# A gated scan feeding a top-1 mixture of experts, on one core: two-operand vector instructions cut in pieces, the start reordered, weights converted in independent parts

## The chip, the cores and the metric

One core of a Trainium2 chip runs the whole program. The metric is the device time of one execution in microseconds (us), as a median over runs. The engines are named as the profile names them: PE (TensorE, matrix multiplication), DVE (VectorE), ACT (ScalarE), POOL (GpSimd), SP (SyncE, which issues most transfers here). Every engine works through its own list of instructions strictly in order; semaphores tie the lists together.

## The reference

```python
# x, r_gate, i_gate: [4, 5056, 256], a_param: [256]
a_base = 1 / (1 + exp(-a_param)); sig_r, sig_i = sigmoid(r_gate), sigmoid(i_gate)
a_t = exp(8 * sig_r * log(clip(a_base, 1e-6, 1 - 1e-6)))          # the decay
x_gated = sqrt(maximum(1 - a_t * a_t, 1e-6)) * sig_i * x
for t in range(S):
    h = a_t[:, t] * h + x_gated[:, t];  y[:, t] = h                # the scan
# y as N = 20224 rows of 256; 8 experts, w1 [8, 256, 1024], w2 [8, 1024, 256]
logits = y @ w_gate + modality_bias[modality_id]                   # top-1 routing
e = argmax(logits);  gate = softmax(logits)[e]
out[row] = gate * (maximum(y[row] @ w1[e], 0) @ w2[e])
```

## The kernel before

**The work.** The scan runs over 23 chunks of time steps (`CHUNKS`): four of 128 steps, 17 of 256, one of 128, one of 64; a chunk holds its steps of all four batches, so chunk 4 and the later long ones give 1024 rows each. Per chunk: three loads `a`, `g`, `x` (the two gates and the input); on ACT two tanh (L507 on `a`, L495 on `g`), two exponentials (L512), a square (L516) and a square root (L518); on DVE the gating product (L498), the product with the root (L520), and the scan itself (L534, `tensor_tensor_scan` over all 2048 columns of a long chunk). Those three DVE instructions read two tensors from the on-chip memory. "Sizing" finds a power of two for the chunk: DVE takes maxima (L669, L678, L683 `mxy`), PE transposes them (L545 into `psz`), DVE and PE answer twice more (L548, L552, L556, L561). With it `y` is split into a high and a low half-precision part (L712 on ACT, L724 on DVE), PE forms the logits (L738, `psl`), DVE routes (L794 to L862, with three small matmuls L832 to L835 in between), SP transposes the rows (L763, `rt`), and POOL scatters them into a table by expert (L885, `rows<-rt,di`, 128 rows an instruction).

**Experts.** Rows are taken from the table in pages of 128 or 256 rows of one expert (`X<-rows` on SP). Below, P0, P1, P2 ... are the pages in PE's order; P0 and P1 have 128 rows, the others 256. Two pages are chosen at a time on DVE (`choose_two`, L985 to L997), one of each of the two experts that the modality bias makes most frequent. A page is layer one (L1197, groups of 12 matmuls into `ph`), ACT and DVE making the two parts of the hidden rows (L1138, L1140), layer two (L1239 into `po`), ACT scaling by the gate (L1149), and POOL writing 128 output rows (L1153). Layer one of a page alternates on PE with layer two of the page before.

**Weights.** The four matrices of the two frequent experts (w0 to w3) come in as f32 and are converted into a high and a low f16 part (`convert`): a scale (16 matmuls L321, then DVE), the high part on DVE (L352), the low part as two matmuls on PE (L368, L369, "a pair" below: four pairs a matrix, 16 in all) and a copy on ACT (L371). The other experts are handled at the end.

**What sets the order.** Nothing waits for a free engine at run time. A planner inside the kernel (`run`) simulates generators that yield (engine, estimated duration, condition, lag) and writes out every engine's list in the order of its own clock; a priority decides among requests that start nearly together. If an estimate is off, an instruction stands too early in its engine's list and all behind it wait. `count["pe"]` also ties each scatter to the last matmul planned ahead of it.

Of the kernel before, what the change touches and what calls it, by code (L numbers as in the profile page):

```python
# [40 lines left out]
HI = "DDDDAD"  # L41
LO = "PPPPDD"
START = "0 w w 1 w w 2"
W_AT = 11.5
C_STEP = 2
GROW = 1.01
EARLY = 8
# [3 lines left out]
W_STEP = 0.1  # L51
# [26 lines left out]
def kernel(  # L78
# [53 lines left out]
    nc.vector.tensor_scalar_add(ch, ch, 1.0)  # L132
    nc.vector.reciprocal(ch, ch)
    nc.vector.tensor_scalar(out=ch, in0=ch, scalar1=1e-6, scalar2=1.0 - 1e-6, op0=ALU.max, op1=ALU.min)
    nc.scalar.activation(ch, ch, AF.Ln)
# [91 lines left out]
    free = {"PE": 0.0, "ACT": 6.0, "DVE": 7.0, "POOL": 9.0, "DMA": 1.0, "queue": 1.0}  # L227
    threads = []
# [108 lines left out]
    def convert(k, name, raw, to, sc):  # L337

        if LO[k] == "P":
            yield "ACT", 0.2, room("dg")  # L340
            td = take("dg")
            dg = sm.tile([P, P], F32, name=f"dg{name}", tag="dg")
            nc.scalar.activation(dg, ident, AF.Copy, scale=sc)
        for v in range(2):
            vs = slice(FF * v, FF * v + FF)
            src, hi, lo = raw[:, vs], to[:, vs], to[:, 2 * FF + FF * v : 3 * FF + FF * v]
            if HI[k] == "A":
# [5 lines left out]
            if LO[k] == "G":  # L353
                yield "POOL", 1.9, None
                nc.gpsimd.tensor_scalar(out=src, in0=src, scalar1=sc, scalar2=None, op0=ALU.mult)
                yield "POOL", 1.9, None, 0.0
                nc.gpsimd.tensor_tensor(out=lo, in0=src, in1=hi, op=ALU.subtract)
                continue
            if LO[k] == "D":
                yield "DVE", 1.2, None  # L360
                nc.vector.scalar_tensor_tensor(out=lo, in0=src, scalar=sc, in1=hi, op0=ALU.mult, op1=ALU.subtract)
                continue
            for h in range(2):
                yield "PE", 1.25, room("ph"), 0.2
                tp = take("ph")
                us = slice(512 * h, 512 * h + 512)
                pl = psh.tile([P, 512], F32, name=f"pl{name}_{v}{h}", tag="ph")
                nc.tensor.matmul(pl, dg, src[:, us], start=True, stop=False)  # L368
# [27 lines left out]
    def hot_weights(m):  # L396
# [12 lines left out]
        yield from convert(m, f"{m}", raw, hw[e][w], sc)  # L409
        give("wr", tr)  # L410
        mark["w", m] = plan["end"]
        tiles["wiv", m] = iv
        if w == 1:
            yield "DVE", 0.07, seen(("w", m - 1)), 0.0
            nc.vector.tensor_tensor(out=hiv[e], in0=tiles["wiv", m - 1], in1=iv, op=ALU.mult)
            mark["hot", e] = plan["end"]

    def cold_weights(pg):
# [11 lines left out]
        for w in range(2):  # L430
# [4 lines left out]
            yield from convert(2 * HOT + w, f"c{pg.c}_{w}", raw[w], pg.w[w], sc)  # L435
            give("wr", t[w])
            if w == 0:
                iv0 = iv
        yield "DVE", 0.07, None, 0.0
# [46 lines left out]

    def done(c, name):

        give(*tickets[c, name])

    def gate_chunk(c):

        z = CHUNKS[c][1] / 256
        yield "ACT", 0.13 + 1.7 * z, seen(("load", c, "g"))
        nc.scalar.activation(tiles[c][1], tiles[c][1], AF.Tanh, scale=0.5)  # L495
        yield "DVE", 0.09 + 2.12 * z, seen(("load", c, "x"))
        a, g, x = tiles[c]
        nc.vector.scalar_tensor_tensor(out=g, in0=g, scalar=1.0, in1=x, op0=ALU.add, op1=ALU.mult)  # L498
        mark["gated", c] = plan["end"]

    def scan_chunk(c):
# [3 lines left out]
        yield "ACT", 0.13 + 1.7 * z, seen(("load", c, "a"))  # L505
        a = tiles[c][0]
        nc.scalar.activation(a, a, AF.Tanh, scale=0.5)  # L507
# [9 lines left out]
        yield "ACT", 0.13 + 1.7 * z + 2.56, None  # L517
        nc.scalar.activation(s, s, AF.Sqrt, scale=-0.25, bias=quarter)  # L518
        yield "DVE", 0.09 + 2.12 * z, None
        nc.vector.scalar_tensor_tensor(out=g, in0=s, scalar=0.5e-3, in1=g, op0=ALU.max, op1=ALU.mult)  # L520
# [12 lines left out]
        yield "DVE", 0.08 + 4.26 * z, None  # L533
        nc.vector.tensor_tensor_scan(out=g, data0=a, data1=g, initial=0.0, op0=ALU.mult, op1=ALU.add)  # L534
# [7 lines left out]
    def power_of_two(name, mx, ng, ps, sc, iv, lag=0.2):  # L542

        yield "PE", 0.06, None
# [4 lines left out]
        yield "DVE", 0.1, None, lag  # L549
# [5 lines left out]
        yield "PE", 0.06 * nd / ng, None  # L555
# [106 lines left out]
    def size_chunk(c):  # L662
# [24 lines left out]
        yield "SP", 0.0, allof(room("lg"), seen("gate")), 0.0  # L687
        tl = take("lg")
# [3 lines left out]
        yield from power_of_two(f"y{c}", mx, B, ps, sc, iv)  # L692
# [172 lines left out]
    def gates(c, l):  # L865
# [3 lines left out]
        yield "ACT", 0.2, None  # L869
# [473 lines left out]
```

## Time and profile before

| | |
|---|---|
| runs | 980.01, 982.94 (median), 983.73 us |
| the profiled execution | 987.79 us, of which the span 986.0 us; 4.85 us above the median |
| busy in the span | PE 919.5 us (93%), DVE 662.3 (67%), ACT 578.6 (59%), POOL 485.1 (49%) |
| PE clock granted | 0.981 of full speed as a mean |
| first matmul of a page (P0) / of the first full page (P2) | 45.88 us / 74.40 us |
| start of the last chunk's scan / of the last row scatter | 645.7 us / 670.8 us |

In the timelines a row gives its start in us, its duration in us, engine, line, operation, output and inputs, how many instructions are merged, and in brackets the idle time of the engine ahead of it and what ended that. In the tables of waits a row gives who waited for whom, the total in us, how often, and the longest. In the tables of one line's instructions stand the number, then the durations in ns as minimum / median / maximum, then the first and last start.

### The profile page before, as it was taken

What the parts mean: (1) busy time and instruction counts of PE and PEld (TensorE: products, weight loads), DVE (VectorE), ACT (ScalarE), POOL (GpSimd) and SP (SyncE); (2) the same over time, 40 slices, a digit from 0 to 9 for tenths busy, and PEclk for the clock granted to TensorE, in tenths of its full rate; (3) what the DMA queues carried; (4) which work ended last, traced back from release to release, by engine and by line L of the source; (5) the groups of instructions that cost most, each with busy time, mean ns of one, the idle gap of its engine ahead of it and who ended that gap; (6) DMA issues with size and microseconds to landing.
All of it is one profiled execution on the core that took longest, in us unless ns stands there. A gap on an engine that the chain in (4) does not pass through costs nothing. (4 is left out here: it accounts for less than half of the span.)

```text
span 986.0 us, 22341 instructions
## 1 busy us (share of the span) xinstructions
PE 919.5 (93%) x8516; PEld 791.1 (80%) x8516; DVE 662.3 (67%) x1564; ACT 578.6 (59%) x819; POOL 485.1 (49%) x539
## 2 busy tenths in 40 slices
PE   3779897899899999999999999999999999999997
PEld 2358686688688888888888888888889888888886
DVE  5888796787899999898888997863523332232321
ACT  7698666575877777775877857643333333333332
POOL 7333563656565777675756767553451111111111
PEclk9899998899999999999999999999999999999999
DMA  7767865678798888877798877644431212212110
GB/s 284 215 204 176 243 218 114 213 192 217 189 252 213 258 235 210 193 200 167 227 247 203 239 175 204 130 113 112 127 92 49 57 49 53 51 49 55 49 39 18
DMA packets 221734, 156.10 MB, mean 158 GB/s; under 512 B 198129, under 2 KB 201330, under 8 KB 215090
## 3 DMA queue, kind: packets, MB, share of 16 engines
q1 hardware_dynamic: 205296, 110.61, 45.7%
q0 software_dynamic: 16176, 43.98, 12.6%
q8 instruction: 68, 1.11, 0.5%
q14 instruction: 48, 0.39, 0.1%
q10 hardware_dynamic: 146, 0.00, 0.0%
HBM read 68.76 MB, written 44.35 MB: 115 GB/s over the span
## 5 line engine op out<-in xcount | busy, mean ns | idle before, releaser
L1197 PE MATMUL ph<-X,hw 128*128 128x256 f16 (+1 forms) x3936 | 480.7, 273 | 8.2 <-DMA X<-rows 8.0
L1239 PE MATMUL po<-hw,H 128*128 128x256 f16 x3840 | 474.2, 274 | 2.3 <-DVE H L1140 1.7
L1197 PEld LDWEIGHTS <-hw 128*128 128x128 f16 x3936 | 379.8, 99 | 59.4 <-DMA X<-rows 8.8
L1239 PEld LDWEIGHTS <-H 128*128 128x128 f16 x3864 | 375.5, 98 | 49.9 <-DVE H L1140 2.5
L1140 DVE SCALAR_TENSOR_TENSOR H<-ph,H 128x512 f16<-128x512 f32 (+1 forms) x332 | 219.2, 668 | 249.8 <-ACT H L1138 198.4
L1138 ACT ACTIVATE H<-ph 128x512 f16<-128x512 f32 (+1 forms) x332 | 191.2, 580 | 275.3 <-PE ph L1197 255.5
L1153 POOL DMA_INDIRECT out_dram<-ot,mt x161 | 197.3, 1226 | 307.0 <-ACT ot L1149 251.9
L885 POOL DMA_INDIRECT rows<-rt,di x158 | 211.8, 1341 | 156.5 <-PE po L1239 50.9
L1149 ACT ACTIVATE ot<-po,gt 128x256 f32<-128x256 f32 x161 | 75.9, 471 | 76.0 <-PE po L1239 51.5
L534 DVE TENSOR_TENSOR_SCAN g<-a,g 128x2048 f32<-128x2048 f32 (+2 forms) x23 | 88.0, 3824 | 0.8
L712 ACT ACTIVATE a<-g,scy 128x512 f16<-128x512 f32 (+2 forms) x92 | 55.8, 655 | 7.4 <-DVE g L534 7.3
L724 DVE SCALAR_TENSOR_TENSOR a<-g,scy,a 128x512 f16<-128x512 f32 (+2 forms) x92 | 58.1, 667 | 0.9 <-ACT a L712 0.9
L512 ACT ACTIVATE a<-a,ch 128x1024 f32<-128x1024 f32 (+2 forms) x46 | 50.5, 1116 | 0.2
L520 DVE SCALAR_TENSOR_TENSOR g<-x,g 128x2048 f32<-128x2048 f32 (+2 forms) x23 | 45.5, 1980 | 2.6 <-ACT x L518 2.5
L498 DVE SCALAR_TENSOR_TENSOR g<-g,x 128x2048 f32<-128x2048 f32 (+2 forms) x23 | 45.9, 1994 | 1.1 <-ACT g L495 1.1
L669 DVE TENSOR_REDUCE top<-x 128x4 f32<-128x2048 f32 (+2 forms) x23 | 45.3, 1971 | 0.4 <-DMA x<-in_x_dram 0.4
L507 ACT ACTIVATE a<-a 128x2048 f32<-128x2048 f32 (+2 forms) x23 | 38.3, 1667 | 8.3 <-DMA a<-in_r_gate_dram 8.2
L516 ACT ACTIVATE x<-a 128x2048 f32<-128x2048 f32 (+2 forms) x23 | 38.4, 1669 | 7.3 <-DVE g L498 7.1
L518 ACT ACTIVATE x<-x,quarter 128x2048 f32<-128x2048 f32 (+2 forms) x23 | 40.5, 1761 | 0.3
L495 ACT ACTIVATE g<-g 128x2048 f32<-128x2048 f32 (+2 forms) x23 | 38.3, 1663 | 1.1 <-DMA g<-in_i_gate_dram 1.0
L518 ACT ACT_TABLE_LOAD x22 | 28.2, 1283 | 0.5
L885 POOL DMA_INDIRECT rows<-nt,ni x16 | 15.5, 972 | 20.8 <-PE po L1239 10.4
(194 smaller groups left out, 464.7 us busy)
## 6 DMA issues: line engine op xcount, KB each, us to landing
a<-in_r_gate_dram SPq DMA_DIRECT2D x17, 1024.0 KB
g<-in_i_gate_dram SPq DMA_DIRECT2D x17, 1024.0 KB
x<-in_x_dram SPq DMA_DIRECT2D x17, 1024.0 KB
wr<-in_moe_w_dram SPq DMA_DIRECT2D x4, 1024.0 KB
out_dram<-ot,mt POOLq DMA_INDIRECT x161
a<-in_r_gate_dram SPq DMA_DIRECT2D x5, 512.0 KB
g<-in_i_gate_dram SPq DMA_DIRECT2D x5, 512.0 KB
x<-in_x_dram SPq DMA_DIRECT2D x5, 512.0 KB
```

Of the source, the lines that this page charges most:

```text
L512: nc.scalar.activation(sl, sl, AF.Exp, scale=ch[:, h : h + 1], bias=ch[:, h : h + 1])
L518: nc.scalar.activation(s, s, AF.Sqrt, scale=-0.25, bias=quarter)
L534: nc.vector.tensor_tensor_scan(out=g, data0=a, data1=g, initial=0.0, op0=ALU.mult, op1=ALU.add)
L712: nc.scalar.activation(ys[:, 0, :, g], yg[:, :, g, :].rearrange("p h (k b) -> p h k b", b=Q), AF.Copy, scale=sc[:, g : g + 1])
L724: nc.vector.scalar_tensor_tensor(out=ys[:, 1, :, g], in0=yg[:, :, g, :].rearrange("p h (k b) -> p h k b", b=Q), scalar=sc[:, g : g + 1], i ...
L885: ins = nc.gpsimd.indirect_dma_start(out=rows[:, :], out_offset=bass.IndirectOffsetOnAxis(ap=idx, axis=0), in_=src, in_offset=None, bounds ...
L1138: nc.scalar.activation(t.H[:, 0, hs, :], ph[:, :, 0:st], AF.Relu)
L1140: nc.vector.scalar_tensor_tensor(out=t.H[:, 1, hs, :], in0=ph[:, :, 0:st], scalar=0.0, in1=t.H[:, 0, hs, :], op0=ALU.max, op1=ALU.subtract,)
L1149: nc.scalar.activation(t.ot[:, a, :], po, AF.Copy, scale=t.gt[:, a : a + 1])
L1153: ins = nc.gpsimd.indirect_dma_start(out=out[:, :], out_offset=bass.IndirectOffsetOnAxis(ap=t.mt[:, a, 0:1], axis=0), in_=t.ot[:, a, :], i ...
L1197: ins = nc.tensor.matmul(ph[:, v, 0:st], lhsT, rhs, start=(m == 0), stop=(m == len(mm) - 1))
L1239: ins = nc.tensor.matmul(po, lhsT, rhs, start=(f == 0 and m == 0), stop=(f == NF - 1 and m == len(mm) - 1))
```

## The change

1. `pieces` and `piece`: from chunk 1 on the DVE instructions with two tensor inputs are cut: the two products in 2, the scan in 4 for a long chunk (1 and 2 for a short one). The planner records these (`held`) and plans a POOL instruction that would start inside one for its end.
2. The start: the tanh of chunk 0 stands ahead of the logarithm of the decay (`decay()`); the bias is loaded ahead of `a_param`; the expert order is computed ahead of `ch`; chunk 1 is loaded ahead of w1 (`START`); the modality order starts at 15 instead of 9 on the planner's clock.
3. Weights: the high parts of w0 and of half of w2 go to ACT (`HI`); each quarter of a low part is a thread of its own (`low(u)`), urgent; the low part of the rare experts' second matrix is cut in four.
4. Planner costs: a table load on ACT (1.28) only where the table changes; a lag of 3.0 (1.0 for chunks 2 to 6) ahead of both of PE's steps in sizing (`SIZE_LAG`); dearer small steps.

```diff
-HI = "DDDDAD"
+HI = ["A", "D", "AD", "D", "A", "D"]
-START = "0 w w 1 w w 2"
+START = "0 w 1 w w w 2"
+MODALITY = 15.0
+SIZE_LAG = 3.0
-W_STEP = 0.1
+W_RANK = [0.0, 0.3, 0.3, 0.6]
...
-    nc.scalar.activation(ch, ch, AF.Ln)
...
+    def decay():
+        yield "ACT", 0.2, seen(("tanh", 0, "a"), ("tanh", 0, "g")), None, "L"
+        nc.scalar.activation(ch, ch, AF.Ln)
...
+                if eng == "POOL":
+                    for b0, b1 in held:
+                        if b0 - 0.1 <= th.start < b1 - 0.1:
+                            th.start = b1 - 0.1
...
+            if eng == "ACT" and len(th.req) > 4 and th.req[4] != table[0]:
+                table[0], dur = th.req[4], dur + 1.28
...
+        def low(u):
+            us = slice(512 * u, 512 * u + 512)
+            src, hi, lo = raw[:, us], to[:, us], to[:, 2 * FF + 512 * u : 2 * FF + 512 * u + 512]
...
+                yield "PE", 1.25, room("ph")
...
             for h in range(2):
-                yield "PE", 1.25, room("ph"), 0.2
...
+                add(low(2 * v + h), prio, plan["end"] + 0.2, urgent)
...
+    def pieces(c, k):
+        return max(1, CHUNKS[c][1] * k // P) if c else 1
+    def piece(t, i, n):
+        w = t.shape[1] // n
+        return t[:, i * w : (i + 1) * w]
...
-        yield "DVE", 0.08 + 4.26 * z, None
-        nc.vector.tensor_tensor_scan(out=g, data0=a, data1=g, initial=0.0, op0=ALU.mult, op1=ALU.add)
+        n = pieces(c, 2)
+        for i in range(n):
+            yield "DVE", 0.08 + 4.26 * z / n, None, 0.0 if i else None, True
+            ai, gi = piece(a, i, n), piece(g, i, n)
+            nc.vector.tensor_tensor_scan(out=gi, data0=ai, data1=gi, initial=0.0, op0=ALU.mult, op1=ALU.add)
...
-    def power_of_two(name, mx, ng, ps, sc, iv, lag=0.2):
-        yield "PE", 0.06, None
+    def power_of_two(name, mx, ng, ps, sc, iv, lag=None):
+        yield "PE", 0.1, None, lag
...
+        lag = SIZE_LAG if c > 6 else SIZE_LAG / 3 if c > 1 else None
...
-    add(modality_order(), (0, 9), 9.0)
+    add(decay(), (0, 0))
+    add(modality_order(), (0, 9), MODALITY)
...
-        add(hot_weights(m), (2, W_AT + W_STEP * m))
+        add(hot_weights(m), (2, W_AT + W_RANK[m]), urgent=True)
```

In the main part DVE gets 1648 instructions instead of 1558 (the scan 78 instead of 23, the two products 40 each instead of 23, the low part of the rare experts' matrix 8 instead of 4, the high parts three fewer), ACT three more; PE, POOL and SP keep theirs. Lines of the changed kernel are some 20 to 50 higher: L507 is L550, L495 is L535, L512 L556, L516 L560, L534 L584, L545 L595, L683 L733, L738 L789, L885 L936, L985 L1036, L1138 L1189, L1153 L1204, L1197 L1248, L1239 L1290, L368 L382, L369 L383.

ACT at the very start, before: `a_246`, `g_248` and `x_250` are chunk 0's tiles, `pm` and `mq` belong to the modality order.

```order
L114 ACT_TABLE_LOAD
L114 ACTIVATE ch<-cpar 128x2
L135 ACT_TABLE_LOAD
L135 ACTIVATE ch<-ch 128x2
L507 ACT_TABLE_LOAD
L507 ACTIVATE a_246<-a_246 128x1024
L512 ACTIVATE a_246<-a_246,ch 128x512 x2
L495 ACTIVATE g_248<-g_248 128x1024
L613 ACTIVATE mq<-pm_281 128x316
L613 ACTIVATE mq<-pm_302 128x316
L516 ACTIVATE x_250<-a_246 128x1024
L518 ACT_TABLE_LOAD
```

The same stretch of ACT after:

```order
L116 ACT_TABLE_LOAD
L116 ACTIVATE ch<-cpar 128x2
L550 ACTIVATE a_241<-a_241 128x1024
L535 ACTIVATE g_243<-g_243 128x1024
L162 ACT_TABLE_LOAD
L162 ACTIVATE ch<-ch 128x2
L556 ACT_TABLE_LOAD
L556 ACTIVATE a_241<-a_241,ch 128x512 x2
L560 ACTIVATE x_245<-a_241 128x1024
L562 ACT_TABLE_LOAD
L562 ACTIVATE x_245<-x_245,quarter 128x1024
```

Both tanh moved ahead of the logarithm and its table, and the two copies of the modality order left the way of the square.

PE where the first page begins, before: `pl` are the pairs of the low parts (`wr_412` is w2), `ph_0_708` is the first group of P0.

```order
L368 MATMUL pl_11_680<-wr_291,dg_472 128x512
L369 LDWEIGHTS nid
L369 MATMUL pl_11_680<-hw_1_225,nid 128x512
L368 MATMUL pl_00_703<-wr_412,dg_668 128x512
L369 LDWEIGHTS nid
L369 MATMUL pl_00_703<-hw_0_226,nid 128x512
L1197 LDWEIGHTS hw_0_224
L1197 MATMUL ph_0_708<-X_664,hw_0_224 128x128
```

PE where the first page begins, after: `wr_420` is w3, `pl_3` its last quarter.

```order
L595 MATMUL psz_774<-identb,mxy_736 4x128
L382 MATMUL pl_2_780<-wr_420,dg_695 128x512
L383 LDWEIGHTS nid
L383 MATMUL pl_2_780<-hw_1_222,nid 128x512
L382 MATMUL pl_3_790<-wr_420,dg_695 128x512
L383 LDWEIGHTS nid
L383 MATMUL pl_3_790<-hw_1_222,nid 128x512
L1248 LDWEIGHTS hw_0_219
L1248 MATMUL ph_0_808<-X_689,hw_0_219 128x128
```

Seven pairs that stood among the matmuls of P0 and P1 now stand ahead of P0: all 16 pairs come first. Chunk 1's logits (`psl`) stand behind 14 pairs instead of 12.

POOL around the rows of chunk 4, before: `rt_0_1806` are its rows, `ot_...` the output rows of pages.

```order
L769 TENSOR_SCALAR rt_0_1806<-tid 128x8
L1153 DMA out_dram<-ot_1885,mt_1450 20224x256
L885 DMA rows<-rt_0_1806,di_1974 164096x258 x3
L1153 DMA out_dram<-ot_1885,mt_1450 20224x256
L885 DMA rows<-rt_0_1806,di_1974 164096x258 x5
L1153 DMA out_dram<-ot_2078,mt_1770 20224x256 x2
```

The same place on POOL after (`rt_0_1902` is chunk 4):

```order
L820 TENSOR_SCALAR rt_0_1902<-tid 128x8
L936 DMA rows<-rt_0_1902,di_2051 164096x258 x4
L1204 DMA out_dram<-ot_2055,mt_1873 20224x256
L936 DMA rows<-rt_0_1902,di_2051 164096x258 x3
L1204 DMA out_dram<-ot_2055,mt_1873 20224x256
L1204 DMA out_dram<-ot_2194,mt_1953 20224x256
L936 DMA rows<-rt_0_1902,di_2051 164096x258
```

Three output writes now stand among the eight row scatters, where one stood.

More of the change, by code (lines that the diff above doesn't have):

```diff
@@ L226 @@
     slots = {t: Slots(n) for t, n in BUFS.items()}
-    free = {"PE": 0.0, "ACT": 6.0, "DVE": 7.0, "POOL": 9.0, "DMA": 1.0, "queue": 1.0}
-    threads = []
+    free = {"PE": 0.0, "ACT": 5.2, "DVE": 7.5, "POOL": 9.0, "DMA": 1.0, "queue": 1.0}
+    threads, held, table = [], [], ["E"]
     plan = {"end": 0.0}
@@ L284, in run @@
             dur = th.req[1]
+            if eng == "ACT" and len(th.req) > 4 and th.req[4] != table[0]:
+                table[0], dur = th.req[4], dur + 1.28
             end = th.start + dur
             free[eng] = end
+            if eng == "DVE" and len(th.req) > 4:
+                held.append((th.start, end))
+                del held[:-4]
             if eng == "DMA":
@@ L408, in hot_weights, with then @@
         yield from scale_of(f"{m}", raw, sc, iv, FACTOR[w])
-        yield from convert(m, f"{m}", raw, hw[e][w], sc)
-        give("wr", tr)
-        mark["w", m] = plan["end"]
         tiles["wiv", m] = iv
+        def then():
+            give("wr", tr)
+            mark["w", m] = plan["end"]
+        yield from convert(m, f"{m}", raw, hw[e][w], sc, (2, W_AT + W_RANK[m]), True, then)
         if w == 1:
@@ L434, in cold_weights, with then @@
             yield from scale_of(f"c{pg.c}_{w}", raw[w], sc, iv, FACTOR[w])
-            yield from convert(2 * HOT + w, f"c{pg.c}_{w}", raw[w], pg.w[w], sc)
-            give("wr", t[w])
+            def then(w=w):
+                give("wr", t[w])
+                mark["cw", pg.c, w] = plan["end"]
+            yield from convert(2 * HOT + w, f"c{pg.c}_{w}", raw[w], pg.w[w], sc, (1, 3), False, then)
             if w == 0:
                 iv0 = iv
-        yield "DVE", 0.07, None, 0.0
+        yield "DVE", 0.07, seen(("cw", pg.c, 0), ("cw", pg.c, 1)), 0.0
         pg.inv = sm.tile([P, 1], F32, name=f"pinv{pg.c}", tag="pinv", bufs=3)
@@ L493, in gate_chunk @@
         z = CHUNKS[c][1] / 256
-        yield "ACT", 0.13 + 1.7 * z, seen(("load", c, "g"))
+        yield "ACT", 0.13 + 1.7 * z, seen(("load", c, "g")), None, "E"
         nc.scalar.activation(tiles[c][1], tiles[c][1], AF.Tanh, scale=0.5)
-        yield "DVE", 0.09 + 2.12 * z, seen(("load", c, "x"))
-        a, g, x = tiles[c]
-        nc.vector.scalar_tensor_tensor(out=g, in0=g, scalar=1.0, in1=x, op0=ALU.add, op1=ALU.mult)
+        mark["tanh", c, "g"] = plan["end"]
+        n = pieces(c, 1)
+        for i in range(n):
+            yield "DVE", 0.09 + 2.12 * z / n, seen(("load", c, "x")), 0.0 if i else None, True
+            a, g, x = [piece(t, i, n) for t in tiles[c]]
+            nc.vector.scalar_tensor_tensor(out=g, in0=g, scalar=1.0, in1=x, op0=ALU.add, op1=ALU.mult)
         mark["gated", c] = plan["end"]
@@ L516, in scan_chunk @@
         nc.scalar.activation(s, a, AF.Square)
-        yield "ACT", 0.13 + 1.7 * z + 2.56, None
+        yield "ACT", 0.13 + 1.7 * z, None, None, "S"
         nc.scalar.activation(s, s, AF.Sqrt, scale=-0.25, bias=quarter)
-        yield "DVE", 0.09 + 2.12 * z, None
-        nc.vector.scalar_tensor_tensor(out=g, in0=s, scalar=0.5e-3, in1=g, op0=ALU.max, op1=ALU.mult)
+        n = pieces(c, 1)
+        for i in range(n):
+            yield "DVE", 0.09 + 2.12 * z / n, None, 0.0 if i else None, True
+            gi, si = piece(g, i, n), piece(s, i, n)
+            nc.vector.scalar_tensor_tensor(out=gi, in0=si, scalar=0.5e-3, in1=gi, op0=ALU.max, op1=ALU.mult)
         done(c, "x")
```

99 lines of the change are left out of this document (53 added, 46 removed).

## The prediction

> **What bounds it.** I read the page first, then PE's table of waits by stretches, then the timelines around the long waits.
>
> ```profile
> PE 919.5 (93%) x8516; PEld 791.1 (80%) x8516; DVE 662.3 (67%) x1564; ACT 578.6 (59%) x819; POOL 485.1 (49%) x539
> ```
>
> PE is the bound of the whole. What can be won is PE's waiting, and what the clock loses behind a wait. The matmuls of pages come in groups of 12, and at full rate they keep a spacing that this stretch shows, as does the slow rate behind a wait:
>
> ```profile
> 45.88 1.48 PE L1197 MATMUL ph<-X,hw 128*128 128x128 f16 x12
> ...
> 52.21 0.41 PE L738 MATMUL psl<-a,wg 128*32 128x128 f16 x16
> ...
> 74.40 8.44 PE L1197 MATMUL ph<-X,hw 128*128 128x256 f16 x60 [1.82 <-DMA X<-rows]
> ...
> 134.64 1.47 PE L1197 MATMUL ph<-X,hw 128*128 128x256 f16 x12
> 135.95 1.47 PE L1239 MATMUL po<-hw,H 128*128 128x256 f16 x12
> ...
> 141.19 6.71 PE L1239 MATMUL po<-hw,H 128*128 128x256 f16 x60
> 153.82 9.66 PE L1197 MATMUL ph<-X,hw 128*128 128x256 f16 x60 [5.91 <-DMA X<-rows]
> ...
> 188.06 0.16 PE L556 MATMUL psz<-dmy,onesb 4*128 4x4 bf16 x1 [3.45 <-issue]
> ...
> 188.18 2.74 PE L1197 MATMUL ph<-X,hw 128*128 128x256 f16 x12
> ...
> 193.27 1.83 PE L1197 MATMUL ph<-X,hw 128*128 128x256 f16 x12
> ```
>
> A group is 1.31 us (135.95 - 134.64). P2 begins at 74.40. P8 begins at 153.82 after 5.91 us without rows, and its first 60 matmuls take 9.66 us where 60 took 6.71 just before: a long wait costs about 3 us more. From P8 on PE is nearly closed, so whatever P8 gains stays to the end. PE's waits between these points and after:
>
> ```profile
> PE ph L1197 <- DMA X<-rows: 6.2, 2, 5.9
> PE psl L738 <- ACT a L712: 2.5, 4, 0.8
> ```
>
> That is 75 to 160 us; from 160 to 700 us it is sizing:
>
> ```profile
> PE psz L545 <- DVE mxy L683: 7.7, 8, 1.6
> PE psz L556 <- issue: 3.6, 2, 3.4
> PE psz L545 <- DVE lm L678: 3.2, 1, 3.2
> PE psz L556 <- DVE dmy L552: 2.6, 5, 0.8
> ```
>
> The 3.4 is the wait at 188.06, and it is no wait of the order: ACT and DVE resume in the same instant, all three put down to no work on this core.
>
> ```profile
> 187.43 0.60 ACT L1138 ACTIVATE H<-ph 128x512 f16<-128x512 f32 x1 [4.14 <-remote]
> 187.47 0.28 DVE L548 TENSOR_REDUCE m1y<-psz 4x1 f32<-4x128 f32 x1 [3.11 <-remote]
> ```
>
> I take it for a pause of this one execution: 3.45 us, and 2.5 behind it (24 matmuls from 188.18 to 193.27, 5.09 instead of 2.62): 6 us, close to the 4.85 by which the profiled execution stands above the median.
>
> **The start, up to P2: 1 us won at most, counted as part of the next term.** Chunk 0's root is limited by ACT:
>
> ```profile
> 4.83 0.20 ACT L114 ACTIVATE ch<-cpar 128x2 f32<-128x2 f32 x1 [1.72 <-DMA cpar<-in_a_param_dram]
> ...
> 7.86 1.06 ACT L507 ACTIVATE a<-a 128x1024 f32<-128x1024 f32 x1
> 8.95 1.52 ACT L512 ACTIVATE a<-a,ch 128x512 f32<-128x512 f32 x2
> ...
> 14.17 1.05 ACT L516 ACTIVATE x<-a 128x1024 f32<-128x1024 f32 x1
> 15.30 1.28 ACT L518 ACT_TABLE_LOAD   x1
> 16.59 1.15 ACT L518 ACTIVATE x<-x,quarter 128x1024 f32<-128x1024 f32 x1
> ```
>
> After: the exponential at 5.3 (a_param now comes second), two tanh of 1.06, a table, the logarithm, a table (1.28, 0.20, 1.28), the two exponentials 1.52, the square 1.05, a table 1.28: the root starts at 14.2, 2.4 us earlier. But P2 hangs on chunk 1, not on chunk 0, and chunk 1's logits stood behind 12 pairs on PE at 52.21 and now stand behind 14, with fewer page matmuls (36 short ones, 2 us) ahead. From about 29.5 us (chunk 0's routing must answer first) 13 pairs follow, at the 1.5 us that two pairs here are apart:
>
> ```profile
> 35.57 1.12 PE L368 MATMUL pl<-wr,dg 128*128 128x512 f32 x2
> ...
> 37.12 1.10 PE L368 MATMUL pl<-wr,dg 128*128 128x512 f32 x2
> ...
> 41.61 1.91 PE L368 MATMUL pl<-wr,dg 128*128 128x512 f32 x2
> ```
>
> 13 x 1.55 and 2 us for w3's and the scales' matmuls give 51.7: the same time. P0 then starts at about 55 instead of 45.88, and the choice of P2 stands on DVE behind P0's and P1's hidden rows and chunk 2's root. I put that choice at 68.5 to 70, where it was:
>
> ```profile
> 69.24 0.20 DVE L985 TENSOR_TENSOR d<-b,u 1x2 f32<-1x2 f32 x1
> ```
>
> The rows arrive some 5 us later in both, so P2 at 73 to 75. Bounds: -5 us if the lead of chunk 0 comes through, +8 if pairs go at the rate of 41.61 (1.91 for two passes instead of 1.1; 13 x 0.6 = 8). The high parts moved to ACT cost 3 x 1.1 there, in ACT's waits for pairs, and relieve DVE; changed `START` delays w1 by 1.5 MB of loads, which nothing waits for before its pairs.
>
> **P2 to P8: 2 us won.** P8 needs chunk 4's rows, which POOL scatters:
>
> ```profile
> 129.84 3.21 POOL L885 DMA_INDIRECT rows<-rt,di  x1 [1.66 <-DVE m1y L548]
> ...
> 137.21 2.08 POOL L885 DMA_INDIRECT rows<-rt,di  x1 [0.30 <-issue]
> 139.59 1.90 POOL L885 DMA_INDIRECT rows<-rt,di  x1 [0.30 <-issue]
> 141.79 0.98 POOL L885 DMA_INDIRECT rows<-rt,di  x1 [0.30 <-issue]
> ...
> 144.37 4.34 POOL L885 DMA_INDIRECT rows<-rt,di  x1 [0.31 <-issue]
> ```
>
> A free scatter takes 0.98, the four long ones 7.6 us more in all. The long ones end 0.8 to 0.9 us after a DVE instruction of two inputs:
>
> ```profile
> 138.35 2.28 DVE L520 SCALAR_TENSOR_TENSOR g<-x,g 128x2048 f32<-128x2048 f32 x1
> ...
> 143.49 4.42 DVE L534 TENSOR_TENSOR_SCAN g<-a,g 128x2048 f32<-128x2048 f32 x1
> ```
>
> 144.37 + 4.34 is 0.80 after the scan's end, 139.59 + 1.90 is 0.86 after L520's. The scatter of 137.21 got through where one such instruction follows on another (it ended at 139.29, inside L520). So a piece should let a scatter through at its end, and the loss per hit falls to a piece's 1.2 us. I take 3 of the 7.6 as left. But two more output writes, taken at a free scatter's 1.29 (0.98 and the 0.30 ahead of it), now stand among the eight: the stretch of 18.9 us becomes 11 x 1.29 + 3 = 17.2. The chunk's logits stood on PE ahead of P6 and still do; its rows start at about 128 instead of 129.84, P8 at 151.5. PE is ready for P8 earlier, since the stalls at chunk 4's logits (2.5) go (their matmuls stand 6.6 instead of 3.9 us of page work behind the last split), and so waits longer there: what is won before P8 is lost at P8. Bounds: 10 won (next part), 8 lost.
>
> **Sizing after P8: 5 us won.** The lag moves PE's two steps back in its list. Counted in groups between the page whose hidden rows stand just ahead of DVE's step and PE's step, the 16 chunks from 7 on have 45 for the first step and 46 for the second before, 50 and 54 after: 14% more, up for some chunks and down for others. Of the 13.5 us (7.7, 3.2, 2.6) and about 1.5 at the slow rate behind the 3.2, I take a third. Bounds: 0 and 15.
>
> **More DVE work: nothing.** A scan of 512 columns takes 1.22, of 2048 4.42; a product of 1024 1.21, of 2048 2.28:
>
> ```profile
> L534 DVE TENSOR_TENSOR_SCAN g<-a,g x23: 1224/4424/4426, 20.2 to 645.7; 128x2048 f32<-128x2048 f32 x17, 128x1024 f32<-128x1024 f32 x5, 128x512 f32<-128x512 f32 x1
> ```
>
> ```profile
> L498 DVE SCALAR_TENSOR_TENSOR g<-g,x x23: 684/2282/2423, 11.4 to 634.6; 128x2048 f32<-128x2048 f32 x17, 128x1024 f32<-128x1024 f32 x5, 128x512 f32<-128x512 f32 x1
> ```
>
> ```profile
> L498 DVE SCALAR_TENSOR_TENSOR g<-g,x 128x1024 f32<-128x1024 f32 x5 | 6.1, 1215 | 1.1 <-ACT g L495 1.1
> ```
>
> 17 x (0.47 + 2 x 0.15) is 13 us on DVE. Between 200 and 650 us DVE has 53 us free:
>
> ```profile
> 200.00:650.00 450.00, 432.71 (x4109) 376.01 (x4107) 396.53 (x886) 330.43 (x435) 300.24 (x259) 1.00 0.79 207
> ```
>
> So it is covered, and a hidden-row step (L1140) no longer stands behind a whole scan; if the cover were gone, PE would wait for L1140.
>
> A rule speaks against the pieces. The Trainium skill ("SBUF — State Buffer", on the shared port pair) says that a DVE instruction with two inputs from that memory and a GpSimd instruction that reads it take the pair as an exclusive lock for a whole instruction, and that whoever comes second blocks fully. By the rule POOL would hold up DVE as well. The trace shows only the one side: L520 at 138.35 kept its 2.28 with a scatter under way, and no scan of 2048 took more than 4426 ns. By the rule the sum would be that of the last rival below; by the trace it stays.
>
> **The sum**, against the profiled execution's own 987.8: -6 for the pause, -2 to P8, -5 in sizing, 0 for DVE: 975, which is 8 under the median of the runs.
>
> **Rivals.**
> - The early lead comes through: P2 3 us earlier, all 7.6 of blocked scatters gone, so P8 10.6 earlier, the wait and the slow rate behind it (3) gone: 987.8 - 6 - 13.6 - 5 = 963. For it: the chain to P8 is a chain of waits, no engine is full there. Against: the choice of P2 stands late, output writes stand among the rows.
> - It does not do what it says: the waits only move, nothing won before P8 or in sizing: 982, the median. For it: the margins in PE's list rise by only 14%, for some chunks they fall.
> - Slower: all pairs ahead of P0, at the slow rate. P2 moves by 8, chunk 4's logits stand in PE's list behind P5, so P8 moves as well: 987.8 - 6 + 8 = 990. It decides if pairs are more than 1.9 apart. For it: PE waits for chunk 0's routing right ahead of them, and went slow behind the wait at 41.61.
> - Slower by DVE: POOL is busy two thirds of the time (300 of 450). If each of 90 more starts waited half a scatter (0.49), DVE would lose 0.67 x 90 x 0.49 = 30 of its 53 free us, and sizing's 13.5 us of waits would grow as the free time shrinks, to 31: 987.8 - 6 - 2 + 17 = 997.
>
> **Chances.** Faster by over 0.5% is under 978.0, slower over 987.9 (about what these runs can tell from no change). The forecast 0.46 (969 to 981: 0.34 faster, 0.12 same), the lead that comes through 0.22, waits that only move 0.15, slow pairs 0.14, the held DVE 0.03. So faster 0.56, same 0.27, slower 0.17. The range 960 to 990 leaves out the lower end of the first rival (0.05), the upper half of the third (0.07) and the last.
>
> **What would show it.** The root of chunk 0 (L562) near 14 us; 16 pairs ahead of P0 at about 55, 1.5 us apart; P2 at 73 to 75; P8 at about 151 with a wait of 8 or more ahead of it; scatters of at most 2.2 us; waits for `mxy`, `lm` and `dmy` of about 9 us in all; DVE busy up by 13. Wrong if P2 comes before 71 or after 78, if P8's wait is gone, or if a scan piece takes much over 1.22.

## The result and the profile after

The changed kernel takes 971.75 us (median of five runs, 969.54 to 975.64); the kernel before has 980.76 in its five. The ratio is 0.9904, 95% interval 0.9874 to 0.9933: faster by 1%. The profiled execution of the changed kernel took 970.82, 17 less than the profiled one before; 6 of these 17 are the pause, which the changed kernel's trace does not have.

The lines of the page that answer to those of before: busy time of the engines, and row scatters and output writes on POOL (busy, mean of one in ns, idle time before). The two POOL lines of before first:

```profile
L1153 POOL DMA_INDIRECT out_dram<-ot,mt x161 | 197.3, 1226 | 307.0 <-ACT ot L1149 251.9
L885 POOL DMA_INDIRECT rows<-rt,di x158 | 211.8, 1341 | 156.5 <-PE po L1239 50.9
```

After:

```profile
PE 913.2 (94%) x8516; PEld 789.8 (82%) x8516; DVE 667.2 (69%) x1654; ACT 581.9 (60%) x822; POOL 433.4 (45%) x539
...
L1204 POOL DMA_INDIRECT out_dram<-ot,mt x161 | 178.1, 1106 | 285.7 <-ACT ot L1200 237.7
L936 POOL DMA_INDIRECT rows<-rt,di x158 | 186.8, 1182 | 210.8 <-PE po L1290 56.7
```

POOL lost 52 us of busy time, 25 of them in scatters and 19 in output writes; DVE gained 5. PE runs the same matmuls, and its busy time falls by 6 of the 17 us: the larger part of the difference is in its waits. The timeline of PE, with P0, P2, P6 and P8:

```profile
48.16 0.83 PE L1248 MATMUL ph<-X,hw 128*128 128x128 f16 x12
...
69.00 6.89 PE L1248 MATMUL ph<-X,hw 128*128 128x256 f16 x36 [2.22 <-DMA X<-rows]
...
121.76 7.08 PE L1248 MATMUL ph<-X,hw 128*128 128x256 f16 x48 [3.09 <-DMA X<-rows]
...
155.02 9.17 PE L1248 MATMUL ph<-X,hw 128*128 128x256 f16 x60 [3.29 <-DMA X<-rows]
```

PE's table of waits from 75 to 160 us, and from 160 to 700 us:

```profile
PE ph L1248 <- DMA X<-rows: 8.6, 3, 3.3
```

```profile
PE psz L595 <- DVE mxy L733: 5.0, 4, 2.1
PE psz L606 <- DVE dmy L602: 4.2, 3, 2.3
```

Where the time went is read best by counting the matmuls of pages on PE, those of both layers: the start of the n-th of them (us).

| n | before | after | lead |
|---|---|---|---|
| 0 (P0) | 45.9 | 48.2 | -2.3 |
| 144 (P2) | 74.4 | 69.0 | 5.4 |
| 336 | 98.3 | 96.5 | 1.8 |
| 720 (P8) | 153.8 | 155.0 | -1.2 |
| 900 | 177.2 | 177.5 | -0.3 |
| 1000 (behind the pause) | 195.4 | 189.5 | 5.9 |
| 1500 | 258.7 | 250.3 | 8.5 |
| 3000 | 436.9 | 428.5 | 8.4 |
| 4500 | 612.0 | 599.5 | 12.5 |
| 7700 | 968.1 | 951.1 | 17.0 |

P2 comes 5.4 us sooner, and all of it is given back before P8. What stays is the pause and some 12 us won a little at a time behind P8.

### The profile page after: what moved, and what is told of

The parts are those of the page before. It is cut to its first block, busy times and chain, and to the rows that moved or that the text cites. A ratio compares the mean times of both kernels' runs of the same rounds, so it can differ in the third digit from the quotient of the medians.

```text
span 969.0 us, 22431 instructions
## 1 busy us (share of the span) xinstructions
PE 913.2 (94%) x8516; PEld 789.8 (82%) x8516; DVE 667.2 (69%) x1654; ACT 581.9 (60%) x822; POOL 433.4 (45%) x539
## 5 line engine op out<-in xcount | busy, mean ns | idle before, releaser
L1248 PE MATMUL ph<-X,hw 128*128 128x256 f16 (+1 forms) x3936 | 478.4, 273 | 10.9 <-DMA X<-rows 10.9
L1290 PE MATMUL po<-hw,H 128*128 128x256 f16 x3840 | 470.9, 273 | 0.4 <-DVE H L1191 0.4
L1248 PEld LDWEIGHTS <-hw 128*128 128x128 f16 x3936 | 379.1, 99 | 59.8 <-issue 7.5
L1290 PEld LDWEIGHTS <-H 128*128 128x128 f16 x3864 | 374.6, 98 | 46.3 <-issue 1.7
L1189 ACT ACTIVATE H<-ph 128x512 f16<-128x512 f32 (+1 forms) x332 | 191.5, 580 | 268.7 <-PE ph L1248 266.6
L1204 POOL DMA_INDIRECT out_dram<-ot,mt x161 | 178.1, 1106 | 285.7 <-ACT ot L1200 237.7
L936 POOL DMA_INDIRECT rows<-rt,di x158 | 186.8, 1182 | 210.8 <-PE po L1290 56.7
L584 DVE TENSOR_TENSOR_SCAN g<-a,g 128x512 f32<-128x512 f32 (+1 forms) x78 | 94.5, 1225 | 0.8
L567 DVE SCALAR_TENSOR_TENSOR g<-x,g 128x1024 f32<-128x1024 f32 (+1 forms) x40 | 48.0, 1199 | 9.5 <-ACT x L562 9.4
L556 ACT ACTIVATE a<-a,ch 128x1024 f32<-128x1024 f32 (+2 forms) x46 | 50.7, 1115 | 0.1
L541 DVE SCALAR_TENSOR_TENSOR g<-g,x 128x1024 f32<-128x1024 f32 (+1 forms) x40 | 48.6, 1218 | 0.0
L550 ACT ACTIVATE a<-a 128x2048 f32<-128x2048 f32 (+2 forms) x23 | 38.3, 1667 | 14.7 <-DMA a<-in_r_gate_dram 14.6
L560 ACT ACTIVATE x<-a 128x2048 f32<-128x2048 f32 (+2 forms) x23 | 38.3, 1666 | 2.8 <-DVE g L541 2.5
L535 ACT ACTIVATE g<-g 128x2048 f32<-128x2048 f32 (+2 forms) x23 | 38.3, 1664 | 0.0
L936 POOL DMA_INDIRECT rows<-nt,ni x16 | 16.0, 997 | 19.8 <-PE po L1290 10.3
```

The costliest lines, as they stand in the source:

```text
L556: nc.scalar.activation(sl, sl, AF.Exp, scale=ch[:, h : h + 1], bias=ch[:, h : h + 1])
L584: nc.vector.tensor_tensor_scan(out=gi, data0=ai, data1=gi, initial=0.0, op0=ALU.mult, op1=ALU.add)
L936: ins = nc.gpsimd.indirect_dma_start(out=rows[:, :], out_offset=bass.IndirectOffsetOnAxis(ap=idx, axis=0), in_=src, in_offset=None, bounds ...
L1189: nc.scalar.activation(t.H[:, 0, hs, :], ph[:, :, 0:st], AF.Relu)
L1204: ins = nc.gpsimd.indirect_dma_start(out=out[:, :], out_offset=bass.IndirectOffsetOnAxis(ap=t.mt[:, a, 0:1], axis=0), in_=t.ot[:, a, :], i ...
L1248: ins = nc.tensor.matmul(ph[:, v, 0:st], lhsT, rhs, start=(m == 0), stop=(m == len(mm) - 1))
```

## The experiments

The theory to test was that of the prediction: the pieces free the scatters, which moves P8; the lag in sizing shortens PE's waits after P8. The rival: the planner wrote another order, and that is all. Kernels are compared with the kernel before by the ratio, since before itself took 980.4 us (median) in the first group of four and 987.8 and 988.5 in the others, each group on another chip; a time in us of a later group (from e5 on) stands 7 to 8 higher, and its stretches may hold a part of that. Two numbers of each profiled execution go into the table: the start of P8, and what is left of the span from there. Before had 826.2 there without its pause of 6. They are numbers of one execution each, which can stand up to 3.5 us off its kernel's median (e2_before_cut: 974.53 against 977.98). The expectations of e9, e11 and e12 count the stretch from P8 to a point some 23 us ahead of the span's end: their 803 for before and 791 for the change are the 826.2 and 814.0 here.

| kernel | ratio (95%) | P8 | P8 to end |
|---|---|---|---|
| before | 1 | 153.8 | 832.2 |
| the change | 0.9904 (0.9874, 0.9933) | 155.0 | 814.0 |
| e1_after_whole | 1.0042 (1.0025, 1.0060) | 156.6 | 825.3 |
| e2_before_cut | 0.9982 (0.9966, 0.9998) | 150.8 | 822.0 |
| e3_after_nolag | 0.9889 (0.9866, 0.9913) | 157.7 | 810.9 |
| e4_before_lag | 0.9879 (0.9859, 0.9898) | 154.0 | 813.7 |
| e5_before_pieces | 0.9960 (0.9943, 0.9978) | 164.1 | 814.4 |
| e6_start_weights | 0.9897 (0.9873, 0.9922) | 157.4 | 816.9 |
| e7_lag_cut | 0.9906 (0.9880, 0.9932) | 153.9 | 821.5 |
| e8_small_steps | 1.0109 (1.0077, 1.0140) | 170.5 | 826.8 |
| e9_lag_two | 0.9964 (0.9944, 0.9984) | 155.3 | 828.8 |
| e10_after_small | 0.9783 (0.9766, 0.9800) | 151.6 | 810.4 |
| e11_two_stages | 0.9930 (0.9912, 0.9947) | 153.8 | 826.4 |
| e12_after_lag3 | 0.9862 (0.9839, 0.9885) | 154.1 | 819.9 |

### The cut alone, with the order kept

Two kernels change no order. The first keeps the changed kernel's order and issues each instruction whole, at its first piece.

```diff
         for i in range(n):
             yield "DVE", 0.08 + 4.26 * z / n, None, 0.0 if i else None, True
-            ai, gi = piece(a, i, n), piece(g, i, n)
+            if i:
+                continue
+            ai, gi = a, g
             nc.vector.tensor_tensor_scan(...)
```

(the same for the two products)

> The changed kernel's order on every engine, but the two products and the scan issued whole, at the place of their first piece; nothing is left out. If the cut is what counts (my theory): the row scatters are blocked again, their sum with the output writes goes from 365 us back to 400 or more, the eight of chunk 4 take 20 us or more instead of 17.7, P8 starts 3 to 5 us after the changed kernel's 155.0, and hidden rows stand behind whole scans: 975 to 979. If the order alone carries the change (rival): scatters longer, but the time within 1.5 us of the changed kernel's 971.75.

The second keeps the order of before and cuts in place:

```diff
         yield "DVE", 0.08 + 4.26 * z, None
-        nc.vector.tensor_tensor_scan(out=g, data0=a, data1=g, ...)
+        n = pieces(c, 2)
+        for i in range(n):
+            ai, gi = piece(a, i, n), piece(g, i, n)
+            nc.vector.tensor_tensor_scan(out=gi, data0=ai, data1=gi, ...)
```

> The kernel before with its own order on every engine, the two products and the scan cut into the pieces of the changed kernel, issued right behind one another; nothing is left out. If the cut is what counts: scatters and output writes fall by some 50 us in sum, the eight of chunk 4 end 4 to 6 us sooner, P8 starts at 148 to 150 instead of 153.8 and the end comes 4 to 6 us sooner: 975 to 977. If the order carries the change: the scatters shorten, P8 moves by less than 2 us, and DVE's 13 us more cancel it: 979 to 982.

Busy time and groups on the page of e1_after_whole, then the same of e2_before_cut:

```profile
PE 918.8 (94%) x8516; PEld 791.1 (81%) x8516; DVE 661.4 (67%) x1565; ACT 581.7 (59%) x822; POOL 482.2 (49%) x539
...
L1210 POOL DMA_INDIRECT out_dram<-ot,mt x161 | 195.2, 1213 | 269.8 <-ACT ot L1206 221.5
L942 POOL DMA_INDIRECT rows<-rt,di x158 | 210.2, 1330 | 190.9 <-PE po L1296 65.2
```

```profile
PE 914.1 (94%) x8516; PEld 789.1 (81%) x8516; DVE 668.7 (69%) x1653; ACT 577.7 (59%) x819; POOL 428.6 (44%) x539
...
L1171 POOL DMA_INDIRECT out_dram<-ot,mt x161 | 177.3, 1101 | 323.0 <-ACT ot L1167 264.4
L903 POOL DMA_INDIRECT rows<-rt,di x158 | 182.3, 1154 | 183.6 <-PE po L1257 65.0
```

That a whole instruction holds up the scatters, and that a piece lets them through, is shown in both directions with the order kept: scatters and output writes go from 364.9 to 405.4 us when the pieces are joined (186.8 + 178.1 to 210.2 + 195.2), and from 409.1 to 359.6 when the whole ones of before are cut (POOL from 485.1 busy to 428.6). What that is worth depends on the order it stands in. In the order written for pieces it is 1.4% (1.0042 against 0.9904): joined, the changed order is slower than before, and slower than either expectation. In the order of before it is 0.2%, between its two expectations, though P8 comes 3 us sooner (4 to 6 were expected):

```profile
150.76 8.39 PE L1215 MATMUL ph<-X,hw 128*128 128x256 f16 x60 [4.42 <-DMA X<-rows]
```

Why 3 and not 6 is seen on the two queues that feed P8: SP's load of its rows in before (the last scatter ahead of it is the one at 144.37 that the prediction shows), then the last scatter and the load in e2_before_cut:

```profile
150.55 1.26 SPq L1118 DMA_TRANSPOSE X<-rows  x1
```

```profile
141.86 0.98 POOL L903 DMA_INDIRECT rows<-rt,di  x1 [0.30 <-issue]
147.39 1.33 SPq L1136 DMA_TRANSPOSE X<-rows  x1
```

The last scatter instruction of chunk 4 ends 5.9 us sooner (142.84 instead of 148.71), but SP's load of P8's rows, whose wait the trace puts down to these scatters, starts only 3.2 sooner: 4.6 us behind that end instead of 1.8. A scatter instruction that ends sooner does not bring its rows sooner by as much.

Where the joined kernel loses, by its waits of PE from 160 to 700 us and by the longest of them, on DVE and on PE:

```profile
PE psz L612 <- DVE dmy L608: 6.7, 6, 3.6
PE psz L601 <- DVE mxy L739: 4.7, 3, 3.6
```

```profile
306.03 2.29 DVE L725 TENSOR_REDUCE top<-x 128x4 f32<-128x2048 f32 x1 [4.31 <-DMA x<-in_x_dram]
...
318.80 4.43 DVE L590 TENSOR_TENSOR_SCAN g<-a,g 128x2048 f32<-128x2048 f32 x1
...
327.02 0.16 DVE L739 SCALAR_TENSOR_TENSOR mxy<-top,lm 128x4 bf16<-128x4 f32 x1
```

```profile
327.24 0.27 PE L601 MATMUL psz<-identb,mxy 128*4 128x128 bf16 x1 [3.63 <-DVE mxy L739]
```

The same step in the changed kernel:

```profile
323.54 0.22 PE L595 MATMUL psz<-identb,mxy 128*4 128x128 bf16 x1 [1.80 <-DVE mxy L733]
```

There the hidden rows of DVE stand between the pieces of the scan, here behind the whole of it; and the maximum over `x` at 306.03 waited 4.31 us for its load, 1.77 in the changed kernel. P8 moved by 1.6 us only, the stretch behind it by 11. So the cost of joining lies in what waits for DVE behind P8, not in P8's rows as I had it; how much of it is the scan's length and how much the loads, these runs don't divide.

### The lag in sizing

> The changed kernel without the lag in sizing (0.2 instead of 3.0 and 1.0 behind PE's two steps); the order is planned anew from chunk 3 on. If the lag is what shortens PE's waits after P8 (my theory): PE's waits for mxy, lm and dmy after 160 us go from 9.2 to 13 or more, and the time to 975 to 978. Rival, the cut DVE instructions let DVE's steps come sooner: waits stay at 8 to 10 us, time 970 to 974.

```diff
-        lag = SIZE_LAG if c > 6 else SIZE_LAG / 3 if c > 1 else None
+        lag = None
```

PE's waits from 160 to 700 us:

```profile
PE psz L606 <- DVE dmy L602: 3.1, 4, 1.1
PE ph L1248 <- DMA X<-rows: 3.0, 1, 3.0
PE psz L595 <- DVE mxy L733: 1.1, 2, 0.7
PE psz L595 <- DVE lm L728: 0.4, 1, 0.4
```

Without the lag the waits for `mxy`, `lm` and `dmy` are 4.6 us, half of those with it and below what either side expected, and the stretch behind P8 is 3 us shorter. So in the changed kernel the lag brings nothing, as the rival said; the time, 969.77, stands at the rival's edge.

> The kernel before with the lag in sizing alone (3.0 from chunk 7 on, 1.0 for chunks 2 to 6, behind PE's two steps). If the lag carries what is won after P8: sizing waits of PE go from 13.5 to about 9, and the time to 974 to 978 with P8 where it was (152 to 156). Rival, the lag helps only together with the pieces: 979 to 983.

```diff
-        yield "PE", 0.06, None
+        yield "PE", 0.06, None, lag
...
         yield "DVE", 0.1, None, lag
...
-        yield "PE", 0.06 * nd / ng, None
+        yield "PE", 0.06 * nd / ng, None, lag
```

(`lag` is 3.0, or 1.0 for chunks 2 to 6.) It was faster than expected, 968.91 us, with its scatters and output writes as long as those of before (227.9 + 177.0). But its edit is not the lag of the change: the argument `lag` of before stands behind DVE's step between PE's two, and the larger value went there too. The exact lag was tried next.

> The kernel before with the lag exactly where the change has it: behind PE's two steps in sizing. (e4_before_lag had it in a third place as well: behind DVE's step between them, so ahead of PE's second.) If the lag behind PE's steps carries the gain after P8: the stretch from P8 to the end is some 10 us shorter than before's 803 (without its pause), and the ratio to before is 0.987 to 0.993 if P8 starts within 2 us of 153.8. Rival, the third place carried it: the stretch is 798 us or more and the ratio 0.994 or more.

The rival held: 0.9964, no shorter behind P8. So the kernel before wins 1.2% with the third place and 0.4% without it. That the third place works as a delay is not shown by this: each of the two is an order planned anew, and e8 below moves as far without an aim. On the changed kernel:

> The changed kernel with the lag in the third place as well (behind DVE's step that feeds PE's second). If PE's waits for dmy (4.2 us after 160 us in the changed kernel) come from a second step that stands right behind DVE's: they go under 1 us and the stretch from P8 to the end falls from 791 us by 3 to 6. Rival, DVE's answers come later too and PE's waits move to mxy and the hidden rows: no shorter, and P8 moves by some us either way with the new order.

```diff
-        yield "DVE", 0.14, None
+        yield "DVE", 0.14, None, lag
```

Waits of PE from 160 to 700 us:

```profile
PE psz L595 <- DVE mxy L733: 12.7, 8, 2.8
```

The waits for `dmy` are gone, as expected, and those for `mxy` went from 5.0 to 12.7: the rival's answer, a wait that changed its place. The ratio, 0.9862, is not distinguishable from the change's.

### The other parts, and an order without an aim

> The kernel before with the pieces planned one by one and POOL planned around them (part 1 of the change alone): the planner orders everything anew. If pieces that other DVE steps can pass between are what wins without the lag (theory): PE's waits on DVE after 160 us fall from 17.2 (without the pause) to 10 or less and the time to 968 to 973, as it was without the lag. Rival, start, weights and planner costs carry that: the time is that of the cut in place, 976 to 980, with 14 us or more of such waits.

> Parts 2, 3 and the small planner costs of the change, without pieces, without POOL planned around them, without the lag. If the pieces carry the gain: 978 to 983, P2 at 69 to 70 all the same, scatters and output writes at 410 us or more in sum. Rival, the new start and weights carry it: 968 to 974.

e5 gives the planner of before the pieces and `held` (part 1 of the diff) and nothing else; e6 is the changed kernel with `pieces` returning 1, `held` not looked at and no lag. Pieces planned alone win 0.4%, start, weights and costs alone 1.0%, with P2 at 68.2 and the scatters as long as before (213.0 + 195.5): the rival holds in both. In e5 PE's waits on DVE after 160 us are still 15 us, 4.6 of them ahead of P8. The stretch of e5 behind P8 is as short as the change's, but P8 stands at 164; ahead of it PE waits for a routing step and for its rows:

```profile
160.84 0.21 PE L856 MATMUL psl<-oh,um 128*128 128x64 f16 x1 [4.62 <-DVE oh L847]
164.12 8.73 PE L1221 MATMUL ph<-X,hw 128*128 128x256 f16 x60 [2.74 <-DMA X<-rows]
```

> The kernel before with three estimates of sizing raised by 0.04 us in the planner (0.06 to 0.10 for PE's two steps, 0.10 to 0.14 for one of DVE's) and nothing else: a change of order without an aim. If an order planned anew gives nothing by itself: 978 to 983. Rival, any new order moves the time by as much as the change did: under 976 or over 985.

```diff
-        yield "PE", 0.06, None
+        yield "PE", 0.1, None
...
-        yield "DVE", 0.1, None, lag
+        yield "DVE", 0.14, None, lag
...
-        yield "PE", 0.06 * nd / ng, None
+        yield "PE", 0.1, None
```

No instruction is added or taken away, three estimates move by a few hundredths of a us, and the kernel is 1.1% slower: as much as the whole change won, so the rival holds. P8 comes 16.7 us later, and that is where the loss is made (the stretch behind it, 826.8, holds an alike pause of its own, shown at the end):

```profile
111.00 2.29 DVE L669 TENSOR_REDUCE top<-x 128x4 f32<-128x2048 f32 x1 [5.71 <-DMA x<-in_x_dram]
```

```profile
116.27 2.31 PE L1239 MATMUL po<-hw,H 128*128 128x256 f16 x10 [5.97 <-DVE H L1140]
...
167.06 0.21 PE L832 MATMUL psl<-oh,um 128*128 128x64 f16 x1 [6.02 <-DVE oh L823]
...
170.52 9.23 PE L1197 MATMUL ph<-X,hw 128*128 128x256 f16 x60 [2.92 <-DMA X<-rows]
```

A maximum over `x` stands on DVE ahead of that chunk's load; hidden rows stand behind it, and PE behind these. The opposite edit on the changed kernel:

> The changed kernel with the three small estimates of sizing put back (0.06, 0.10, 0.06 per step): the opposite of e8_small_steps, an order planned anew without an aim. If what the change won is robust: ratio to before 0.987 to 0.994. Rival, it depends on the order that the planner happens to write: above 0.997 or below 0.984, with the difference made before P8.

It gave the best kernel of all, 966.83 us against 988.49 (0.9783), better than before by 2.2% and than the change by 1.2%. So here too the rival holds by the time, though the difference to the change is made on both sides of P8: P8 comes at 151.6, 3.4 us sooner than in the change, and the stretch behind it is 3.6 shorter.

### Do two stages add up?

> The kernel before with the lag, and the same order with the three DVE instructions cut, the pieces right behind one another. If what the cut does (rows of chunk 4 sooner) and what the lag does (PE's waits after P8) add up: 968.9 less 2 to 5, 964 to 967, with P8 at 150 to 152. Rival, P8 doesn't hang on the scatters' durations any more once the lag moved the order: 968 to 971.

> The kernel before with the cut in place for chunks 1 to 6 only (PE's order is that of before until after P8) and the lag in three places as in e4_before_lag, but from chunk 7 on only. If the time is two stages that add up (P8 hangs on the scatters of chunk 4, the rest on DVE's steps in sizing): P8 at 150 to 151.5 instead of 153.8, then 790 to 794 us from P8 to the end: ratio 0.982 to 0.987, better than the change. Rival, the stages don't add up: ratio 0.988 or more.

They don't. e7 is e4 with the cut of e2; 0.9906 against 0.9879, with intervals that overlap, shows no gain from the cut there. e11 has the cut of e2 for chunks 1 to 6 and e4's lag from chunk 7 on. P8 stands at 153.8, where e2 had 150.8, though chunk 4's scatters take 14.4 us from the first to the end of the last instead of the 18.9 of before:

```profile
130.82 3.05 POOL L905 DMA_INDIRECT rows<-rt,di  x1 [1.66 <-DVE dmy L571]
...
144.23 0.98 POOL L905 DMA_INDIRECT rows<-rt,di  x1 [0.30 <-issue]
149.47 1.61 SPq L1138 DMA_TRANSPOSE X<-rows  x1
```

They start 1 us later than in before (130.82 instead of 129.84), the rows' load starts 4.3 us behind the last of them (1.8 in before, 4.6 in e2), and P8 starts 4.3 us behind the load (3.3 in before): nearly all of the 4.5 us is gone. Behind P8 PE waits for `mxy` again:

```profile
PE psz L564 <- DVE mxy L702: 11.4, 8, 2.6
```

## Why the prediction was right, and where its steps were not

The time (975 forecast, 971.75 measured), the sign and the range held. The sum in the profiled execution was 13 and came out as 17. That it came so near is luck: up to P8 2 us were forecast as won and 1.2 were lost, behind P8 (without the pause) 5 were forecast and 12 won, and the two misses partly cancel. Two of its own signs speak against its account of the way to P8: P2 came before 71 ("wrong if"), and the wait ahead of P8 was 3.3 us, not 8 or more. Step by step:

**The pause: right.** It costs 6.2 us between the 900th and the 1000th page matmul, forecast 6: before takes 18.2 us for these 100 matmuls, the change 12.1, and e2, which has the order of before, 11.9.

**The start: wrong.** P0 came at 48.2, not 55, and P2 at 69.0, not 73 to 75. The pairs began at 25.92, not 29.5, and went like this:

```profile
41.13 1.02 PE L382 MATMUL pl<-wr,dg 128*128 128x512 f32 x2
...
42.20 1.02 PE L382 MATMUL pl<-wr,dg 128*128 128x512 f32 x2
```

They are 1.07 apart. The 1.5 came from two pairs of before that had small matmuls of a scale between them, the 1.91 from pairs behind a wait for a high part of DVE's:

```profile
36.75 0.50 PE L328 MATMUL pt<-ss,onesf 128*128 128x1 f32 x4
...
41.23 0.58 PE L369 MATMUL pl<-hw,nid 128*128 128x512 f16 x1 [3.01 <-DVE hw L352]
```

Of the first the changed order has less, of the second nothing: between 25 and 48 us PE waits once, 0.7 us, and not for a pair. The choice of the next two pages came at 62.08 instead of 69.24. The root of chunk 0 came at 15.21, not 14.2: `cpar`, loaded second, arrived at 6.31, not 5.3, and both tanh stand behind its exponential on ACT.

**P2 to P8: wrong in size, and the step that failed is the chain behind it.** I had 2 us won up to P8; from P2 to P8 6.6 were lost, the 5.4 that P2 brought and 1.2 more. The scatters of chunk 4 behave as forecast (17.7 us from the first to the end of the last, forecast 17.2), but start late, at 132.32 and not at 128:

```profile
132.32 1.05 POOL L936 DMA_INDIRECT rows<-rt,di  x1 [10.14 <-DVE H L1191]
...
148.84 1.18 POOL L936 DMA_INDIRECT rows<-rt,di  x1 [0.30 <-issue]
```

The rows of DVE tell why, as far as rows can; no run changes this place alone. Chunk 4's routing is cut in two by two hidden-row steps of P6, and P6 itself waits for its rows until 121.76:

```profile
122.91 0.23 DVE L874 TENSOR_TENSOR oh<-ky,mx 128x64 f16<-128x64 f32 x1
124.45 0.69 DVE L1191 SCALAR_TENSOR_TENSOR H<-ph,H 128x512 f16<-128x512 f32 x1 [1.32 <-ACT H L1189]
126.88 0.69 DVE L1191 SCALAR_TENSOR_TENSOR H<-ph,H 128x512 f16<-128x512 f32 x1 [1.74 <-ACT H L1189]
127.49 0.28 DVE L878 TENSOR_TENSOR_SCAN cu<-rmask,oh 128x64 f16<-128x64 f16 x1
```

4.3 us pass between two routing steps. PE's lead turned into longer waits for rows (8.6 us instead of 6.2), and the late page then held up the routing of the next rows, a loop that I had not followed. The first rival, 963 by a lead that comes through, failed at this place: the lead came at P2 and did not reach P8.

**Sizing behind P8: right in direction, too small, and the cause that I gave is wrong.** The waits for `mxy`, `lm` and `dmy` fell from 13.5 to 9.2 us, as forecast (9). But the stretch behind P8 gained 12 (832.2 less the pause, 814.0), not 5: the waits for hidden rows, for `last` and the unnamed ones went too (3.6 in all, without the pause), so did the 1.4 at the conversion of a rare expert's weights, and the rest, 3 us, is less busy time of PE for the same matmuls (802.7 us behind P8 in before, 2.5 of it lost behind the pause, 797.2 after), of which no run shows the cause. And it isn't the lag. The lag also stands otherwise than I wrote: the fourth entry of a request delays the step that follows it, so the lag comes behind PE's two steps and delays DVE's answers, where the description of the change has it ahead of PE's steps. Without it the changed kernel is as fast (e3), and with it alone before wins 0.4% (e9).

**More DVE work: right in the price.** Pieces cost 11.7 us (scans 94.5 instead of 88.0, products 96.6 instead of 91.4), forecast 13, and PE didn't visibly pay. DVE's busy time as a whole rose by 4.9 only, not by 13; the three high parts fewer are 2 of that difference. A scan piece keeps its duration beside a free-running POOL (ns, minimum, median, maximum; the 2293 is chunk 0's whole scan):

```profile
L584 DVE TENSOR_TENSOR_SCAN g<-a,g x78: 1185/1215/2293, 17.7 to 614.7; 128x512 f32<-128x512 f32 x77, 128x1024 f32<-128x1024 f32 x1
```

So the two-sided lock of the Trainium skill ("SBUF — State Buffer", the shared port pair) did not decide the time: POOL is held up by DVE, as e1 and e2 show with the order kept, and no scatter is seen to hold up DVE: the 77 cut pieces of the scan last at most 1.23 us. But the prediction read the other side of the lock as absent, and it is not. POOL's own instructions with two tensor inputs (`bm`, `bn`) lengthen a product beside them. The longest such case in the changed kernel, DVE's row (both halves of a product merged) and then POOL's:

```profile
117.88 2.66 DVE L541 SCALAR_TENSOR_TENSOR g<-g,x 128x1024 f32<-128x1024 f32 x2
```

```profile
117.90 0.31 POOL L704 TENSOR_TENSOR bm<-mf,mb 128x64 f32<-128x64 bf16 x1
118.16 1.30 POOL L704 TENSOR_TENSOR bn<-mg,mb 128x64 f32<-128x64 bf16 x1
```

The two halves take 2.66 us instead of 2.4, and `bn`, 0.31 when free, takes 1.30. Five products of the changed kernel last 1.3 us or more instead of 1.22, all of them beside such an instruction; that is 0.7 us in all, too little to matter. The last rival is out.

**What stays open.** The gain does not divide into the parts of the change. Alone they give 0.4 (pieces), 0.4 (lag) and 1.0% (start, weights and costs), the three small estimates cost about 1.1 to 1.2% in two kernels, and each of these is one order of many that the planner could have written. That another order alone can move the time by as much as the change is shown (e8, e10); which part of the change's own 1% is its pieces and which its order is not: joining the pieces loses 1.4% there (e1), and the kernel without any pieces wins 1.0% (e6). That the estimates are wrong in size, or that 0.06 is nearer to the truth than 0.10, isn't shown: both pairs moved the same way, and two orders are no sample. Which of the changed order's rows make its 12 us behind P8 was not tried.

## What to carry to other kernels

Where a planner writes every queue's order, give it an edit without an aim (an estimate moved by a few hundredths) before crediting a change: here that moved the time by 1.1%, as much as the change. To price one part, hold the order and change the instruction (cut in place, joined in place); the same cut was worth 1.4%, 0.2% and nothing in three orders. And follow a lead to the next wait for data: a page that starts sooner may only wait longer for its rows.

## What the hardware showed that was not expected

A scatter issued by POOL stays unfinished while DVE works on an instruction with two tensor inputs and ends within a us of its end; instructions a half or a quarter as long took scatters and output writes from 409 us in all to 360 to 365. Scatters left DVE's instructions as they were, within 0.1 us; POOL's own instructions with two tensor inputs made products up to 0.2 us longer. And a scatter that ends sooner as an instruction need not have its rows in place sooner: the load behind it started 1.8 us after it in before, 4.6 in e2.

An alike wait of several engines at once came twice. It is the pause of before (3.45 us on PE), which did not come at the same place in e2 with the same order, and it came at 218 us in e8_small_steps:

```profile
218.35 0.47 ACT L1149 ACTIVATE ot<-po,gt 128x256 f32<-128x256 f32 x1 [5.35 <-remote]
218.51 0.28 DVE L548 TENSOR_REDUCE m1y<-psz 4x1 f32<-4x128 f32 x1 [3.52 <-remote]
```

What ended these waits, no trace says.
